# Window attention feeding a channel-mixing layer: probabilities turned over in 32x32 blocks on VectorE, their products with the values on 32x64 parts of the array

## The chip, the cores and the metric

The kernel runs on one core of a Trainium2 chip. The core's engines have their own instruction queues and run beside each other: TensorE (PE in the profile, its weight loads PEld), VectorE (DVE), ScalarE (ACT), GpSimd (POOL) and SyncE (SP, which issues the DMAs here). The metric is the device time of one execution in microseconds. Lower is better.

## The reference

Attention over 8 batches and 8 heads, 512 local and 32 global tokens of head size 64, in fp32. A global query attends to all 544 keys; a local query attends to the 32 global keys (scores `s_lg`) and to local keys at a distance of at most `window` = 32. The result, 8 x 544 tokens of 512 channels, goes through a gated channel-mixing layer in which each token is blended with the one before it.

```python
k_all = np.concatenate([k_g, k_l], axis=2)
v_all = np.concatenate([v_g, v_l], axis=2)
s_g = scale * np.matmul(q_g, k_all.transpose(0, 1, 3, 2))
out_g = np.matmul(sm(s_g), v_all)
mask = np.abs(pos[:, None] - pos[None, :]) <= window
s_ll = np.where(mask, s_ll, -1000000000.0)
s_l = np.concatenate([s_lg, s_ll], axis=-1)
out_l = np.matmul(sm(s_l), np.concatenate([v_g, v_l], axis=2))
...
xk = mu_k * x + (1.0 - mu_k) * x_prev
xr = mu_r * x + (1.0 - mu_r) * x_prev
k = np.maximum(xk @ w_k, 0.0)
v = k * k @ w_v
r = 1.0 / (1.0 + np.exp(-(xr @ w_r)))
return r * v
```

## The kernel before

**Units and blocks.** A unit is one batch and two heads (`Unit`, four per batch); units are worked on in pairs, 16 pairs in all. The 512 local queries are cut into 16 blocks of 32 (`CK`). A block of queries needs a window of four 32-key blocks (`W` = 128 keys): its neighbours, itself and the global block, which is repeated in the order of the keys (`ORDER`, L30) so that every window is a plain slice. There are 14 different windows (`NW`), and two blocks at either end share theirs.

**Scores.** `scores` (L345) makes, for a pair, 128 products on 64x32 parts of the array into four PSUM banks `ps_s`. DVE adds the mask and takes the minimum (L368, one instruction for 128 queries and 128 keys), ACT takes the exponential with the row sum (L374), DVE inverts the sum (L332, L333), POOL multiplies (L380). `scores_global` (L425) does the same for the 2 x 2 x 32 global queries of a pair against 544 keys, in two banks. The probabilities lie in `Pt` and `Pg` with queries on partitions.

**Turning them over.** For the product with the values the keys have to lie on partitions. `transposes` (L407) turns four 128x128 pieces of `Pt` over on TensorE into one PSUM bank `ps_t` (L144), and ACT copies the bank into the tile `PT` (L414, L418). `transposes_global` (L469) does so for `Pg` in six pieces, in two parts, with copies at L478 and L484. In `PT` each group of four query blocks has a row of 128 columns with room behind it (`PITCH`, `TAIL`) for global queries that need the same window.

**Weighted sums.** `weighted` (L488) takes, for each unit, window and head, the window's values as the stationary side (128 keys x 64 channels, a slice of `raw_v`) and the probabilities of all blocks with this window as the moving side, 32, 64 or 96 columns: 112 products for a pair on two column halves of the array, one for each head, into three banks. Each product finishes its output but for the global queries, which add up over the windows. ACT then copies the sums into `xT` and `xg_all` (L529 to L545). The array `v` therefore holds all 14 windows of both heads, 896 KB a unit, laid out on the host.

**The channel-mixing layer.** It works on half a batch of local tokens (`TOK` = 256) at a time. All matrices are split into a high and a low part, so that each product is three matmuls of 128x128 weights with 256 columns (L141, into `ps_m`, three banks). The steps `F` below are 24 such products each. DVE and POOL prepare its inputs (L609 to L619 the blend of a token with the one before; L733 to L741 sums, differences and splits) and take its results (L808 to L835).

**Order.** Up to the loop over the batches (L1183) a scheduler places the instructions; in it TensorE's are kept in program order by hand (`line["on"]`), and those of ACT, DVE and POOL too (`manual_schedule`, L1180). `batch` (L1068) yields the steps of the layer for one batch, `attention` (L876) those of the heads of the next, and `in_turn` (L939) takes them as the string in `BATCH` (L1172) says, A for attention and F for the layer. After an F it also issues one entry of the list `softmaxes`: exponentials and normalising of the pair's scores, spread over the following turns. For a pair the A steps before are four of `transposes`, one for each part of `transposes_global` (the second with the scores of the next pair behind it) and one with the global scores and `weighted`. The first batch goes in halves, with the weights being loaded and decoded beside it.

```python
        None: "AFAFAFAFAF" "AFFAFF" "AFAFAFAFAF" "AFFFAFF",
```

## Time and profile before

| | |
|---|---|
| three runs | 654.7, 662.81 and 659.24 us, median 659.24 |
| the profiled execution | span 655.7 us from its first to its last instruction; its page gives no other time for it |
| mean granted TensorE clock | 0.995 |
| TensorE | busy 96% of the span, 8362 matmuls and as many weight loads |
| transposes of probabilities on TensorE (L144, from `Pt` and `Pg`) | 256 + 16 of 128x128 and 80 of 96 rows |
| weighted sums (from `PT` and `raw_v`) | 1840 products recorded |
| DMA | 127.15 MB, queue of the program busy 54.6% of 16 engines' span |

The profile has several views. The page gives busy time and share of each engine, and groups of instructions with their count, busy time (overlaps counted once), mean duration and the idle time of the engine before them, with what ended it. Mean durations of matmuls contain their way through the array, so they are longer than the spacing of one start to the next. The chain is the work that ended last, followed back from the end. The windows give busy times by stage, and the timeline the instructions in order.

### The profile page before, as it was taken

What the parts mean: (1) busy time and instruction counts of PE and PEld (TensorE: products, weight loads), DVE (VectorE), ACT (ScalarE), POOL (GpSimd) and SP (SyncE); (2) the same over time, 40 slices, a digit from 0 to 9 for tenths busy, and PEclk for the clock granted to TensorE, in tenths of its full rate; (3) what the DMA queues carried; (4) which work ended last, traced back from release to release, by engine and by line L of the source; (5) the groups of instructions that cost most, each with busy time, mean ns of one, the idle gap of its engine ahead of it and who ended that gap; (6) DMA issues with size and microseconds to landing.
All of it is one profiled execution on the core that took longest, in us unless ns stands there. A gap on an engine that the chain in (4) does not pass through costs nothing.

```text
span 655.7 us, 20533 instructions
## 1 busy us (share of the span) xinstructions
PE 630.7 (96%) x8362; PEld 599.6 (91%) x8362; DVE 510.9 (78%) x1308; ACT 338.4 (52%) x1062; POOL 348.4 (53%) x318
## 2 busy tenths in 40 slices
PE   6789899999999989999999999999999999999998
PEld 3567889999989989989999999989999999999997
DVE  4699986556898677986989698986898687787980
ACT  4888686637263576464463727364745533314111
POOL 6377775334856242764357443855366535652840
PEclk9799999999999999999999999999999999999999
DMA  9826534538366922727555584737383562462774
GB/s 333 353 98 241 177 137 163 170 111 307 128 218 208 332 95 73 278 57 289 204 214 190 193 303 163 240 110 267 136 288 103 190 229 67 144 227 79 240 232 170
DMA packets 43565, 127.15 MB, mean 194 GB/s; under 512 B 4048, under 2 KB 20944, under 8 KB 43472
## 3 DMA queue, kind: packets, MB, share of 16 engines
q1 hardware_dynamic: 43472, 125.85, 54.6%
q8 instruction: 66, 1.08, 0.6%
q14 instruction: 27, 0.22, 0.1%
HBM read 108.53 MB, written 17.30 MB: 192 GB/s over the span
## 4 chain that ended last, share of the span: by engine, by line
PE 78%; DVE 10%; DMA 4%; ACT 3%; POOL 2%; issue 2%; SPq 1%; DVEq 0%; ACTq 0%; POOLq 0%
PE ps_m L141 60%; PE ps_s L141 12%; PE ps_t L144 4%; DMA w<-w_k 2%; DMA w<-w_v 1%; DVE diff L614 1%; DVE xfull L582 1%; PE ps_t L141 1%; POOL wv_l L240 1%; ACT Pt L374 1%; DVE a L272 1%; DVE ps_s L230 1%; DVE ps_s L227 1%; DVE kkl L641 1%; DVE bh L740 1%
## 5 line engine op out<-in xcount | busy, mean ns | idle before, releaser
L141 PE MATMUL ps_m<-xkh,wk_h 128*128 128x256 f32 x544 | 155.6, 286 | 2.7 <-DVE gate L685 0.9
L141 PE MATMUL ps_m<-xkl,wk_h 128*128 128x256 f32 x544 | 151.6, 279 | 1.2 <-POOL xkl L587 1.2
L141 PE MATMUL ps_m<-xkh,wk_l 128*128 128x256 f32 x544 | 150.9, 278 | 0.0
L141 PE MATMUL ps_m<-bh,a 128*128 128x256 f32 x736 | 137.3, 283 | 0.0
L380 POOL TENSOR_TENSOR Pt<-Pt,ssum 128x512 f32<-128x512 f32 x64 | 69.6, 1093 | 89.5 <-DVE ssum L333 45.5
L141 PEld LDWEIGHTS ps_m<-bh,a 128*128 128x128 f32 x736 | 115.0, 189 | 0.0
L141 PEld LDWEIGHTS ps_m<-xkh,wk_h 128*128 128x128 f32 x544 | 102.2, 188 | 8.5 <-issue 2.4
L374 ACT ACTIVATE Pt<-Pt,m 128x128 f32<-128x128 f32 x256 | 99.2, 390 | 16.8 <-DVE m L368 16.5
L141 PEld LDWEIGHTS ps_m<-xkl,wk_h 128*128 128x128 f32 x544 | 102.5, 188 | 2.1 <-POOL xkl L587 1.4
L141 PE MATMUL ps_m<-bl,a 128*128 128x256 f32 x368 | 103.0, 280 | 0.0
L141 PEld LDWEIGHTS ps_m<-xkh,wk_l 128*128 128x128 f32 x544 | 102.4, 188 | 0.0
L656 ACT ACTIVATE relu<-ps_m 128x512 f32<-128x512 f32 x52 | 31.0, 596 | 90.3 <-PE ps_m L141 89.8
L141 PE MATMUL ps_m<-xrh,wr_h 128*128 128x256 f32 x272 | 77.0, 283 | 0.0
L141 PE MATMUL ps_m<-xrl,wr_h 128*128 128x256 f32 x272 | 75.6, 278 | 0.0
L141 PE MATMUL ps_m<-xrh,wr_l 128*128 128x256 f32 x272 | 75.4, 278 | 0.0
L619 POOL TENSOR_TENSOR xkl<-xfull,xkh 128x512 fp32r<-128x512 f32 x30 | 39.7, 1325 | 66.5 <-DVE ssum L332 43.1
L141 PEld LDWEIGHTS ps_m<-bl,a 128*128 128x128 f32 x368 | 69.6, 189 | 0.0
L414 ACT COPY PT<-ps_t 128x512 f32<-128x512 f32 x56 | 32.8, 585 | 67.7 <-PE ps_t L144 67.7
L619 POOL TENSOR_TENSOR xrl<-diff,xrh 128x512 fp32r<-128x512 f32 x30 | 40.7, 1356 | 46.8 <-DVE xrh L618 29.8
L368 DVE CUSTOM_DVE_ANT_0 Pt<-ps_s,masks 128x128 f32<-128x128 f32 x256 | 55.9, 285 | 12.0 <-PE ps_s L141 12.0
L141 PE MATMUL ps_s<-raw_qk 64*32 64x128 f32 (+1 forms) x2112 | 55.4, 287 | 5.4 <-DMA raw_qk<-qk 5.4
L741 POOL TENSOR_TENSOR bl<-B,bh 128x512 fp32r<-128x512 f32 x36 | 51.9, 1459 | 14.3 <-DVE bh L740 13.9
(128 smaller groups left out, 1522.1 us busy)
## 6 DMA issues: line engine op xcount, KB each, us to landing
a<-scratch SPq DMA_DIRECT2D x92, 512.0 KB, 4.8
raw_v<-v SPq DMA_DIRECT2D x32, 896.0 KB, 7.6
raw_qk<-qk SPq DMA_DIRECT2D x32, 624.0 KB, 5.5
out_l<-gate SPq DMA_DIRECT2D x32, 256.0 KB, 4.1
w<-w_k SPq DMA_DIRECT2D x8, 512.0 KB, 9.4
w<-w_v SPq DMA_DIRECT2D x8, 512.0 KB, 4.1
w<-w_r SPq DMA_DIRECT2D x4, 512.0 KB, 3.2
scratch<-wv_h SPq DMA_DIRECT2D x8, 256.0 KB, 3.8
```

What stands on the lines that cost most here:

```text
L141: return in_line(nc.tensor.matmul(*a, **kw))
L144: return in_line(nc.tensor.transpose(*a, **kw))
L227: nc.vector.tensor_scalar(bits, word(I32, 1), 3, 0x7FFFFFF8, op0=ALU.logical_shift_left, op1=ALU.bitwise_and)
L230: nc.vector.scalar_tensor_tensor(bits, word(I32, 1), -(2 ** 31), bits, op0=ALU.bitwise_and, op1=ALU.bitwise_or)
L240: engine.tensor_sub(lo, val, hi.bitcast(F32))
L368: read = nc.vector.tensor_tensor_reduce(out=Pt[:, i], in0=place(t, n, h), in1=masks[:, 2 * slots[t][1] + n], op0=ALU.add, op1=ALU.min, sca ...
L374: nc.scalar.activation(Pt[:, i], Pt[:, i], AF.Exp, bias=low_x[:, i:i + 1], scale=-1.0, accum_out=ssum[:, i:i + 1],)
L380: nc.gpsimd.tensor_mul(Pt[:, some], Pt[:, some], inv.unsqueeze(2).to_broadcast([P, 4, W]))
L414: copy(pitched(j, h, 0, 4), tp.rearrange("p (g q) -> p g q", g=4))
L619: nc.gpsimd.tensor_sub(lo[:, both], xf, hi[:, both].bitcast(F32))
L656: nc.scalar.activation(rk, kp, AF.Relu)
L741: (nc.vector if b[0] == "B" else nc.gpsimd).tensor_sub(l, val, h.bitcast(F32))
```

## The change

- **Turning over on VectorE.** `transposes` and `transposes_global` go. `turn_over` transposes `Pt` on DVE straight into `PT`, 128 x 512 in one instruction, and `turn_over_global` all of `Pg` (128 x 544). DVE's transpose works inside blocks of 32x32: block (r, c) of queries and keys stays in its row of blocks, so the keys of a block lie on the partitions 32r to 32r + 31 of the query block's row r. The PSUM bank and ACT's copy between are gone.
- **Products on 32x64 parts.** A key block's product now contracts 32 keys on row quarter r with one head's 64 channels: for each unit 4 groups x 4 key blocks x 4 row quarters x 2 heads, with 32 moving columns, or 64 where the same values also serve a global query block that lies on this quarter. Four key blocks add up in PSUM. Key blocks that a quarter does not have for its global queries (`MORE`, four for each quarter) come as extra products. Row quarter r writes its own bank of `ps_s`, four banks in all.
- **Values.** `v` holds each key block on the row quarters that use it, and the extra blocks: 2304 values a partition in place of 1792, 1152 KB a unit.
- **Copies out.** For each unit ACT copies two pieces for the global queries, one column, and four pieces of local sums.
- **Order.** The scores of the global queries use banks of `t` and `m`. Where the order is by hand, the five transposes of the next pair are spread over the turns after `weighted`, in front of a turn's normalising. The qk loads are issued one pair earlier, after `weighted` and ahead of the v loads. A pair has two A steps there (seven before): the scores, and the global scores with `weighted`; in `BATCH` the five alternating turns become five F.
- **First batch.** Waits for the last transpose become waits for matmuls that keep the clock up (8 and 24 of them).

```diff
+NG = 4
+ROWS = tuple(tuple(NG * g + r for r in range(NG)) for g in range(NG))
+
+
+def blocks_of(i):
+    at = START[window_of(i)] // CK
+    return ORDER[at:at + NG]
+
+
+OWN, MORE = [], []
+for r in range(NG):
+    own = {}
+    for g in range(NG):
+        for n, m in enumerate(blocks_of(ROWS[g][r])):
+            own.setdefault(m, (g, n))
+    MORE.append([m for m in range(NCK) if m not in own])
+    OWN.append({cell: m for m, cell in own.items()})
+CELLS = [m for m in range(NCK - 1)] + [None, NCK - 1]
+N_MORE = max(len(m) for m in MORE)
...
-NV = 2 * NW * D
+PW = 2 * 2 * NG * W
+LV = NG * NG * 2 * D
+NV = LV + N_MORE * D
...
+    PT = const.tile([P, PW + CK * len(CELLS)], F32, name="PT")
...
-        s.v = raw.rearrange("p (h w d) -> p h w d", h=2, d=D)
+        s.v = raw[:, :LV].rearrange("p (g n h d) -> p g n h d", g=NG, n=NG, h=2)
+        s.more = raw[:, LV:].rearrange("p (e d) -> p e d", d=D)
...
+    def part_of(j, h, g=0, n=0):
+        return (((j * 2 + h) * NG + g) * NG + n) * CK
+
+    def turn_over(r, h, j=None):
+
         if j is not None:
-            copy(pitched(j, h, 0, 4), tp.rearrange("p (g q) -> p g q", g=4))
+            at = part_of(j, h)
+            nc.vector.transpose(PT[:, at:at + NG * W], r.Pt[:, 4 * h:4 * h + 4].rearrange("p i w -> p (i w)"))
         else:
-            g0 = 2 * r.slots[0][1]
-            out = PT[:, :, h, g0 * PITCH:(g0 + 2) * PITCH].rearrange("p j (g q) -> p j g q", g=2)[:, :, :, 0:W]
-            copy(out, tp.rearrange("p (j g q) -> p j g q", j=2, g=2))
-        return last
-
+            for t in range(2):
+                at, i = part_of(t, h, 2 * r.slots[0][1]), 4 * h + 2 * t
+                nc.vector.transpose(PT[:, at:at + 2 * W], r.Pt[:, i:i + 2].rearrange("p i w -> p (i w)"))
+
+    def turn_over_global(Pg):
+        nc.vector.transpose(PT[:, PW:], Pg)
...
-    def scores_global(units, bank="o", other="t", later=False):
+    def scores_global(units, bank="t", other="m", later=False):
...
+    def weighted(units, xTs, PG=None, halves=range(2)):
+
+        banks = [psum("s") for _ in range(NG)]
         begun = set()
 
-        def groups(j, of):
-            s = units[j]
-            for w, here, t in GROUPS:
-                here = [i for i in here if i in blocks]
-                t = t if PG else None
-                if not here and t is None or ((here or [None])[0] in alone) != (of is alone):
-                    continue
-                for h in range(2):
-                    P_of, out = PT[:, j, h], (rest if of is alone else sums)[j][h * D:(h + 1) * D]
-                    if len(here) == 1 and t is not None:
-                        i, = here
-                        moving = cells(P_of, PLACE[i], TAIL[t] - PLACE[i], 2)
-                        out = cells(out, of.index(i) * CK, (of.index(None) - of.index(i)) * CK, 2)
-                    else:
-                        x, y = [PLACE[i] for i in here], [of.index(i) * CK for i in here]
-                        if t is not None:
-                            x, y = x + [TAIL[t]], y + [of.index(None) * CK]
-                        n, x, y = len(x) * CK, min(x), min(y)
-                        moving, out = P_of[:, x:x + n], out[:, y:y + n]
-                    first = of is alone or (out.tensor.name, h) not in begun
-                    begun.add((out.tensor.name, h))
-                    last = matmul(out, s.v[:, h, w], moving, start=first, stop=True, skip_group_check=True)
-        groups(0, shared)
-        groups(0, alone)
-        groups(1, alone)
-        groups(1, shared)
+        def product(j, r, h, v, cell, local, m):
+            at, to = [], []
+            if local:
+                at.append(cell)
+                to.append(j * P + cell[0] * CK)
+            if m is not False:
+                at.append(CELLS.index(m))
+                to.append(2 * P + j * CK)
+            at = [part_of(j, h, *x) if isinstance(x, tuple) else PW + x * CK for x in at]
+            rows, out = slice(r * CK, (r + 1) * CK), banks[r][h * D:(h + 1) * D]
+            if len(at) == 2:
+                moving = cells(PT[rows], at[0], at[1] - at[0], 2)
+                out = cells(out, to[0], to[1] - to[0], 2)
+            else:
+                moving, out = PT[rows, at[0]:at[0] + CK], out[:, to[0]:to[0] + CK]
+            matmul(out, v[rows], moving, start=(r, h) not in begun, stop=True, skip_group_check=True)
+            begun.add((r, h))
+        for j, s in enumerate(units):
+            for g in range(NG):
+                local = g // 2 in halves
+                for n in range(NG):
+                    for r in range(NG):
+                        for h in range(2):
+                            m = OWN[r].get((g, n), False) if PG and r == 2 * j + h else False
+                            if local or m is not False:
+                                product(j, r, h, s.v[:, g, n, h], (g, n), local, m)
+            if PG:
+                for e in range(N_MORE):
+                    for h in range(2):
+                        r = 2 * j + h
+                        product(j, r, h, s.more[:, e], None, False, MORE[r][e])
...
+                for h in range(2):
+                    rows = slice(h * D, (h + 1) * D)
+                    nc.scalar.copy(
+                        xg_all[rows, s.c, s.b, 1:SG + 1], banks[2 * j + h][rows, 2 * P + j * CK:2 * P + (j + 1) * CK]
+                    )
+                nc.scalar.copy(xT[:, 0:1], xg_all[:, s.c, s.b, SG:SG + 1])
+            g0, n = NG // 2 * halves[0], NG // 2 * len(halves)
+            for r in range(NG):
+                x = xT[:, 1 + (g0 * NG + r) * CK:]
+                one = x[:, :CK]
+                read = nc.scalar.copy(
+                    bass.AP(one.tensor, one.offset, (one.ap[0], (NG * CK, n), (1, CK))),
+                    banks[r][:, j * P + g0 * CK:j * P + (g0 + n) * CK].rearrange("p (g q) -> p g q", q=CK),
+                )
...
+        for s in pairs[1]:
+            load_qk(s)
+        over = False
+        for pair, nxt, after in zip(pairs, pairs[1:] + [None], pairs[2:] + [None] * 2):
             xTs = [xT_of(s.b, s.c) for s in pair]
-            for s in nxt or ():
-                load_qk(s)
-            for j, r in enumerate(R):
-                for h in range(2):
-                    transposes(r, h, j)
+            by_hand = line["all"]
+            if not over:
+                for j, r in enumerate(R):
+                    for h in range(2):
+                        turn_over(r, h, j)
+                turn_over_global(Pg)
+                if not by_hand:
                     yield
-            transposes_global(Pg, (0,))
-            yield
-            transposes_global(Pg, (1,))
-            by_hand = line["all"]
             if nxt:
                 R = [scores(whole(s), by_hand) for s in nxt]
                 if by_hand:
@@ -908,14 +886,24 @@
             if nxt:
                 Pg, *softmax = scores_global(nxt, later=True)
             copied = weighted(pair, xTs, True)
+            over = by_hand
             if nxt:
                 if by_hand:
-                    softmaxes.append((norm[3], softmax[0]))
-                    softmaxes.append((softmax[1],))
+                    done = 3 - len(softmaxes)
+                    rest = [*softmaxes, (norm[3], softmax[0]), (softmax[1],)] + [()] * 2
+                    turns = [lambda k=k: turn_over(R[k // 2], k % 2, k // 2) for k in range(4)]
+                    turns.append(lambda: turn_over_global(Pg))
+                    for k, f in enumerate(turns):
+                        at = max(k + 1 - done, 0)
+                        rest[at] = (f, *rest[at])
+                    softmaxes.clear()
+                    softmaxes.extend(x for x in rest if x)
                 else:
                     with tc.issue_after(copied.ins):
                         for f in softmax:
                             f()
+            for s in after or ():
+                load_qk(s)
...
+        turn_over_global(Pg[i])
+        warm = keep_warm((8, 24)[i], warm)
+        with tc.issue_after(warm.ins):
...
-        None: "AFAFAFAFAF" "AFFAFF" "AFAFAFAFAF" "AFFFAFF",
+        None: "FFFFF" "AFFAFF" "FFFFF" "AFFFAFF",
...
+    k_all = in_order(k_l, k_g)
+    of_block = lambda m: v_g if m is None else v_l[:, :, m * CK:(m + 1) * CK]
+    v = np.zeros((B, C, NG, CK, NV), v_l.dtype)
+    for r in range(NG):
+        for g in range(NG):
+            for n, m in enumerate(blocks_of(ROWS[g][r])):
+                x = of_block(m).reshape(B, C, 2, CK, D)
+                for h in range(2):
+                    at = ((g * NG + n) * 2 + h) * D
+                    v[:, :, r, :, at:at + D] = x[:, :, h]
+        for e, m in enumerate(MORE[r]):
+            x = of_block(m).reshape(B, C, 2, CK, D)
+            v[:, r // 2::2, r, :, LV + e * D:LV + (e + 1) * D] = x[:, r // 2::2, r % 2]
+    v = v.reshape(B, C, P, NV)
```

More of the change, by code (lines that the diff above doesn't have):

```diff
@@ L463, in cells @@
         return bass.AP(one.tensor, one.offset, (one.ap[0], (step, n), (1, size)))
-    def tails(rows, at, step, n):
-        first = PT[rows, 0, 0, at:at + CK]
-        return bass.AP(first.tensor, first.offset, (first.ap[0], (PART, 4), (step, n), (1, CK)))
-    def transposes_global(Pg, parts=(0, 1), fill=(0, 0)):
-        copies = []
-        for part in parts:
-            ts = ((0, 1, 5), (2, 3, 4))[part]
-            tp = psum("t")[:, :3 * P].rearrange("p (t n) -> p t n", n=P)
-            for n, t in enumerate(ts):
-                lo, hi = (t * (W - CK), (t + 1) * (W - CK)) if t < 5 else (NGK - W, NGK)
-                last = transpose(tp[:hi - lo, n], Pg[:, lo:hi], ident)
-            n, rows = (2 if 5 in ts else 3), slice(0, W - CK)
-            nc.scalar.copy(
-                tails(rows, TAIL[ts[0]], TAIL[ts[1]] - TAIL[ts[0]], n),
-                tp[rows, 0:n].rearrange("p t (u q) -> p u t q", u=4),
-            )
-            if 5 in ts:
-                rows = slice(P - 2 * CK, P)
-                nc.scalar.copy(tails(rows, TAIL[5], CK, 1), tp[rows, 2:3].rearrange("p t (u q) -> p u t q", u=4))
-            last = keep_warm(fill[part], last)
-        return last
@@ L984, in all_transposes @@
         for h in range(2):
-            last = transposes(r, h)
-        return last
+            turn_over(r, h)
     load_qk(heads_0[0])
@@ L1005, in local_global_attention_then_rwkv_ffn @@
     R, Pg = [], []
-    for pair, bank in zip(pairs_0, "os"):
+    for i, pair in enumerate(pairs_0):
         R.append(by_halves(pair, 0))
-        if bank == "o":
-            Pg.append(scores_global(pair, bank, bank))
+        if i == 0:
+            Pg.append(scores_global(pair, "t", "t"))
             keep_warm(10, scores_global.last)
@@ L1012, in local_global_attention_then_rwkv_ffn @@
             with tc.issue_after(keep_warm(16, R[1].made).ins):
-                Pg.append(scores_global(pair, bank, bank))
+                Pg.append(scores_global(pair, "t", "t"))
+        warm = scores_global.last
         next(decoding)
@@ L1016, in local_global_attention_then_rwkv_ffn @@
         all_transposes(R[i])
-        final = transposes_global(Pg[i], fill=((0, 8), (16, 8))[i])
-        with tc.issue_after(final.ins):
+        turn_over_global(Pg[i])
+        warm = keep_warm((8, 24)[i], warm)
+        with tc.issue_after(warm.ins):
             weighted(pair, xTs_0[i], True, (0,))
@@ L1033, in local_global_attention_then_rwkv_ffn @@
     for i, pair in enumerate(pairs_0):
-        final = all_transposes(R[2 + i])
-        with tc.issue_after(final.ins):
-            weighted(pair, xTs_0[i], None, (1,))
+        all_transposes(R[2 + i])
+        weighted(pair, xTs_0[i], None, (1,))
         next(decoding)
```

58 lines of the change are left out of this document (3 added, 55 removed).

## The prediction

> **What bounds the kernel now.** I read the page's busy line first, then the chain of work that ended last in one stretch of the steady part, then busy times by stage.
>
> ```profile
> span 655.7 us, 20533 instructions
> PE 630.7 (96%) x8362; PEld 599.6 (91%) x8362; DVE 510.9 (78%) x1308; ACT 338.4 (52%) x1062; POOL 348.4 (53%) x318
> ```
>
> TensorE is busy for 96% of the span. One pair of units, from its scores to the next pair's, reads in the chain (start, duration, what):
>
> ```profile
> 390.35 1.98 PE ps_s L141 x123
> 392.33 8.37 PE ps_m L141 x72
> 400.70 0.27 PE ps_t L141 x4
> 400.97 4.27 PE ps_s L141 x116
> 405.24 5.66 PE ps_m L141 x48
> 410.89 0.44 PE ps_t L144 x4
> 411.33 2.83 PE ps_m L141 x24
> 414.16 0.44 PE ps_t L144 x4
> 414.60 2.74 PE ps_m L141 x24
> 417.34 0.44 PE ps_t L144 x4
> 417.77 2.83 PE ps_m L141 x24
> 420.61 0.44 PE ps_t L144 x4
> 421.04 2.74 PE ps_m L141 x24
> 423.79 0.33 PE ps_t L144 x3
> 424.11 2.74 PE ps_m L141 x24
> 426.85 0.33 PE ps_t L144 x3
> 427.18 1.98 PE ps_s L141 x127
> ```
>
> There is nothing but TensorE in it, so here each microsecond off TensorE's queue is a microsecond off the kernel, until another engine takes over. The transposes (L144) stand in that queue six times: 4 x 0.44 + 2 x 0.33 = 2.42 us per pair. The 4.27 us hold the global scores and the weighted sums; the sums alone appear in the last pair, which has no successor (the 3.61 us row below).
>
> Who could take over? The windows give span, then busy PE, PEld, DVE, ACT, POOL:
>
> ```profile
> 0.00:109.00 109.00, 92.45 (x1375) 76.92 (x1375) 88.90 (x277) 82.13 (x265) 74.86 (x102) 0.97 0.60 224
> 109.00:154.00 45.00, 44.98 (x769) 42.75 (x769) 23.45 (x104) 22.18 (x87) 16.19 (x15) 1.00 0.39 134
> 154.00:226.70 72.70, 71.61 (x1001) 68.92 (x997) 57.90 (x150) 35.17 (x114) 43.27 (x39) 1.00 0.68 238
> 226.70:284.40 57.70, 54.17 (x659) 52.08 (x660) 47.51 (x107) 34.10 (x105) 29.13 (x23) 1.00 0.45 158
> 261.30:284.40 23.10, 22.15 (x198) 21.78 (x198) 22.54 (x36) 11.21 (x31) 18.10 (x14) 1.00 0.72 250
> 390.35:462.00 71.65, 71.16 (x998) 68.67 (x998) 59.73 (x159) 38.32 (x126) 38.48 (x30) 1.00 0.59 207
> ```
>
> The last row is one whole batch (two pairs) of the steady part: TensorE full, DVE 59.73 of 71.65 us. DVE is the second bound, and the change gives it work.
>
> **The change part by part.**
>
> ```profile
> 541.20 3.61 PE ps_s L141 x112
> L141 PE MATMUL ps_s<-PT,raw_v 128*64 128x32 f32 x896 | 28.2, 222 | 0.4 <-DVE m L368 0.4
> L141 PE MATMUL ps_s<-PT,raw_v 128*64 128x64 f32 x448 | 18.1, 222 | 0.2 <-issue 0.2
> L414 ACT COPY PT<-ps_t 128x512 f32<-128x512 f32 x56 | 32.8, 585 | 67.7 <-PE ps_t L144 67.7
> L822 DVE TENSOR_TENSOR sum<-ps_m,sum 128x512 f32<-128x512 f32 x6 | 4.1, 691 | 13.1 <-PE ps_m L141 13.1
> L741 DVE TENSOR_TENSOR bl<-B,bh 128x512 fp32r<-128x512 f32 x40 | 53.2, 1331 | 1.4
> L380 POOL TENSOR_TENSOR Pt<-Pt,ssum 128x512 f32<-128x512 f32 x64 | 69.6, 1093 | 89.5 <-DVE ssum L333 45.5 <-ACT Pt L374 21.6 <-PE ps_t L141 10.6
> ```
>
> *Transposes leave TensorE*: -2.42 us per pair, all of it on the path. With them go the ACT copies out of ps_t (0.585 us each); ACT is busy 38.32 of 71.65 us, so this counts as nothing.
>
> *Weighted sums*. Before: 112 products in 3.61 us, two column halves at a time, 32.2 ns each. After, by the code: per unit 4 groups x 4 key blocks x 4 row quarters x 2 heads = 128, and 4 extra blocks x 2 heads = 8; two units, 272. No row shows a product on a 32x64 part. Lower end: a half takes 64.5 ns per product now, and eight parts working freely give 64.5 / 8 = 8.1 ns, 2.2 us in all. Upper end: no more overlap than today, 272 x 32.2 ns = 8.8 us. The nearest row is that of the scores: they also use eight parts (64x32) and need 1.98 us for the code's 128 products (127 recorded), 15.5 ns each. I take that: 272 x 15.5 ns = 4.21 us, +0.60 us per pair, net -1.82. The same two rows show that halving the width saves nothing: products 32 and 64 wide both take 222 ns. [...]
>
> *Transposes come to DVE*: per pair four of 128x512 and one of 128x544. Before has no such row. Nearest with one pass over 512 elements: 691 ns (L822, reads PSUM). Far end: 1331 ns, an operation from SBUF to SBUF that lies beside POOL. Below 691 lies half of it, if DVE moved two elements at a time. I take 0.69 and 0.73 us, so 3.5 us per pair, 7.0 per batch. [...]
>
> DVE would then need 59.73 + 7.0 = 66.7 us per batch; TensorE 71.65 - 2 x 1.82 = 68.0. What DVE idles now is mostly waiting, and later work takes those gaps only where it is late anyway:
>
> ```profile
> 373.97 0.43 DVE L618 CAST xrh<-diff 128x512 fp32r<-128x512 f32 x1 [2.62 <-PE ps_m L141]
> 377.36 0.69 DVE L822 TENSOR_TENSOR sum<-ps_m,sum 128x512 f32<-128x512 f32 x1 [2.66 <-PE ps_m L141]
> 396.67 0.29 DVE L368 CUSTOM_DVE_ANT_0 Pt<-ps_s,masks 128x128 f32<-128x128 f32 x1
> ```
>
> In the first pair of a batch the transposes fall right into the 2.62 and 2.66 us that DVE waits for TensorE; in the second DVE runs on without such a gap. I leave 2.0 us of the 11.9 idle us that DVE cannot fill: 68.7 us per batch, DVE setting it, a gain of 2.95. Bounds: 68.0 and 71.65.
>
> *New waits*. A transpose waits for POOL's normalising (1093 ns) and blocks everything behind it on DVE, among it the additions that free ps_m. The order in the diff puts it one turn of 24 products (2.74 us) behind that multiplication, so I charge nothing; without that cover it is up to 1.1 us for each of five. The weighted sums now write all four ps_s banks from the start, so they wait for all sixteen reductions L368. These ended at 396.96, the sums began after 400.97: 4 us of cover, gone if DVE falls that far behind. One ps_m bank serves the global scores; it is free again after a short DVE read.
>
> ```profile
> PE ps_t L144 <- ACT PT L418: 5.3, 2, 4.5
> PE ps_t L144 <- POOL Pt L380: 3.4, 2, 2.1
> ```
>
> TensorE's own waits for the softmax (these two rows) go, since no transpose stands in its line; what is late next is the weighted sum, several products later.
>
> *DMA, SP's queue*. `v` grows from 896 to 1152 KB, and qk loads move one pair forward, ahead of the v loads. In the steady part a pair has over 30 us to land: nothing. At the start two v loads go out ahead of the third weight chunk:
>
> ```profile
> raw_v<-v SPq DMA_DIRECT2D x32, 896.0 KB, 7.6
> GB/s 333 353 98 241 177 137 163 170 111 307 128 218 208 332 95 73 278 57 289 204 214 190 193 303 163 240 110 267 136 288 103 190 229 67 144 227 79 240 232 170
> 4.94 14.89 DMA w<-w_k
> ```
>
> 512 KB more at 340 GB/s (first two slices) is 1.5 us on a chunk that is on the chain. POOL loses its clearing of PT, and ACT has four more small copies per pair: hidden by idle ACT.
>
> **The sum**, against the 655.7 us span. 0 to 109: +1.5 for DMA; DVE, busy 88.90 of 109, takes some 7 us more of half-size transposes, of which I charge 2, less 1.5 for TensorE's waits on ACT's copy: +2.0 (ends -4, +7). 109 to 154: two pairs, DVE half idle: 2 x -1.82 = -3.6. 154 to 226.7: two pairs, but the first one's five transposes stand together before its scores; half of 3.5 us comes back: -2.0. 226.7 on: two pairs, TensorE's wait for POOL saves another 1.5, and in 261.3 to 284.4, where DVE is full (22.54 of 23.10), 3.5 us come straight on: -1.5. The last seven pairs, 3.5 batches: 3.5 x -2.95 = -10.3. After 541.20 nothing. Sum -15.4: span 640.3. The median of the runs, 659.24, stands 3.5 above the profiled span; so 643.8 us.
>
> **The rivals.**
> - *DVE eats the gain.* It falls so far behind that the gaps are not found again: the last seven pairs, and those from 154 to 284, gain nothing. For it: 22.54 of 23.10. Against: the two gaps above. -3.6 + 2.0 gives a span of 654.1, 657.6 us.
> - *Slower: parts do not overlap.* 8.8 us in place of 3.61 is +5.2 - 2.42 = +2.7 per pair, 14 pairs and the start: about +40, 699 us. It turns slower once a product takes over (3.61 + 2.42) / 272 = 22 ns. Against it: 15.5 ns in the scores.
> - *Slower: DVE's transposes share a path with POOL* and cost 1.33 us as L741 does: a batch needs 59.73 + 13.4 + 2.0 = 75.1, +3.5 each, +12 over 3.5 batches; 154 to 226.7 +1, the next +3, the start +6, 109 to 154 -3.6: about +19, 678 us. It turns slower above (71.65 - 2.0 - 59.73) / 10 = 0.99 us.
> - *More: eight parts run freely*, 2.2 us: TensorE gains 3.8 per pair, DVE still holds the steady part at -10.3; -7.6, -4, -3.5 and +2 elsewhere: -23.4, 635.8 us.
>
> **How the numbers follow.** Two per cent (13 us: faster below 646.1, slower above 672.4) is about what a measurement of this kernel can tell from no change. My forecast has 0.47 (its own range 636 to 653, about 0.12 of it on the near side of 646), more 0.13, DVE eats the gain 0.24, DVE beside POOL 0.11, no overlap 0.05. Faster 0.35 + 0.13 = 0.48; same 0.12 + 0.24 = 0.36; slower 0.16. From 634 to 672 leaves out half of "more" (0.06) and nearly all that is slower (0.14).
>
> **What would show it.** Right: no L144 but the warm-up ones, weighted sums of about 4.2 us, DVE transposes of 0.65 to 0.75 us, batches of about 68.7 us with DVE over 95% busy, and chain pieces on DVE where there are none now. Wrong: transposes near 1.3 us beside POOL; weighted sums over 6 us; TensorE waiting for ps_s before the sums; DVE still idle while batches last 68.0, which would say that its waits gave way more than I allow.

## The result and the profile after

The changed kernel takes 875.54 us (median of four runs, 874.0 to 876.42), beside 660.8 us for the kernel before in the same measurement (654.7 to 662.81): ratio 1.3291, 95% interval 1.3203 to 1.338. The prediction was 643.8 us, in a range of 634 to 672. It was wrong, and by more than its slowest rival (699).

The page of the changed kernel, its head and the lines of the queues, the chain and one group:

```profile
span 873.9 us, 33725 instructions
PE 722.6 (83%) x14970; PEld 685.3 (78%) x14970; DVE 538.5 (62%) x1396; ACT 301.2 (34%) x1018; POOL 345.2 (40%) x312
...
PEclk9666786969796978879696978969696979789999
...
q8 instruction: 117, 1.92, 0.8%
...
PE 71%; issue 16%; DVE 7%; DMA 3%; ACT 2%; POOL 1%; SPq 0%; DVEq 0%; ACTq 0%; POOLq 0%
...
L150 PE MATMUL ps_s<-PT,raw_v 32*64 32x32 f32 (+1 forms) x8800 | 153.9, 266 | 121.6 <-issue 117.1
```

No engine took over: every engine is busy for a smaller share than before, TensorE 83% in place of 96%. The new piece of the chain is "issue", 16% of the span: an engine waits, and for nothing that the profile shows. The group says where: 117.1 us of it stand in front of the weighted sums. Two counts are to be noted. The sums have 8800 records (a record is one matmul in the trace, with its weight load), where the code has 4400 products. And the kernel has 13,192 instructions more (33725 - 20533), while the queue that brings instructions moves 0.84 MB more than before:

```profile
q8 instruction: 66, 1.08, 0.6%
```

That is 64 bytes for each new instruction (0.84 MB / 13,192), and the bytes are those of TensorE alone: its 2 x 14970 loads and matmuls at 64 bytes make the 1.92 MB. A packet of it holds 16.4 KB (1.92 MB / 117).

The timeline of TensorE through one pair's weighted sums in the changed kernel (start, duration, line, operation, count, and in brackets the idle time before with what ended it):

```profile
461.47 2.11 PE L150 MATMUL ps_s<-PT,raw_v 32*64 32x64 f32 x183
467.43 2.67 PE L150 MATMUL ps_s<-PT,raw_v 32*64 32x64 f32 x128 [3.85 <-issue]
471.18 2.14 PE L150 MATMUL ps_s<-PT,raw_v 32*64 32x32 f32 x128 [1.07 <-issue]
476.29 2.45 PE L150 MATMUL ps_s<-PT,raw_v 32*64 32x32 f32 x105 [2.97 <-issue]
```

The stage takes 17.27 us where 4.21 were forecast and 3.63 stood. It has 544 records for 272 products. TensorE runs 183 of them at 11.5 ns, stops for nearly 4 us, and from then on works in portions of exactly 128 records. A record is a weight load and a matmul, so a portion is 256 instructions, 16 KB at 64 bytes each: one packet. In the stretch from 461 to 479 us the queue has four packets, which make 0.07 MB:

```profile
q8 instruction: 4, 0.07, 1.4%
DMA  0005679999960000100009089999600000001000
```

The second line is the busy share of the DMA engines in 40 slices of 0.45 us, in tenths. The packets start at 465.0, 468.5, 474.0 and 477.4 us. The three portions (467.43, 471.18 and 476.29) each begin 2.3 to 2.7 us after one of the first three. The third packet comes 5.4 us after the second: from about 471.4 to 474 us the kernel's own loads keep the DMA engines full.

The windows of the same stretch (span, then busy PE, PEld, DVE, ACT, POOL with counts, granted clock, DMA share, GB/s): the first burst, the rest of the sums, and the 168 feed-forward products behind them.

```profile
461.47:463.58 2.11, 2.11 (x185) 2.01 (x184) 1.73 (x3) 1.89 (x9) 1.29 (x2) 1.00 0.41 84
463.58:478.68 15.10, 7.21 (x362) 6.91 (x361) 2.71 (x11) 0.81 (x5) 2.26 (x2) 0.55 0.42 156
478.68:499.60 20.92, 20.92 (x169) 20.82 (x168) 19.17 (x31) 6.54 (x19) 14.15 (x10) 0.91 0.63 220
```

While TensorE stops and goes, the granted clock falls to 0.55, and the feed-forward products behind it still pay: 20.92 us for 168, where the chain before had 8.37 us for 72, or 19.5 for as many. It takes no long gap for that: in a later stage of the same kernel, where no gap is longer than 1.88 us, the clock falls too.

```profile
705.84:708.57 2.73, 2.73 (x246) 2.61 (x245) 2.61 (x6) 1.93 (x9) 1.77 (x2) 1.00 0.03 9
710.44:714.18 3.74, 2.31 (x128) 2.15 (x128) 3.08 (x6) 0.00 (x0) 1.51 (x2) 0.57 0.48 160
```

What came out as forecast are VectorE's transposes:

```profile
L419 DVE STREAM_TRANSPOSE PT<-Pt 128x512 f32<-128x512 f32 x56 | 37.4, 693 | 22.4 <-PE ps_s L150 21.0 <-POOL xkl L596 1.4
L426 DVE STREAM_TRANSPOSE PT<-Pg 128x544 f32<-128x544 f32 x16 | 11.7, 732 | 5.0 <-PE ps_s L150 4.5 <-POOL Pg L459 0.5
```

To place the loss, the span is cut at the starts of the weighted sums of pair 3 (the first that is not halved), of pair 5 (the first in the part ordered by hand) and of pair 16, the last. This table holds the runs below as well; us, from the timelines.

| kernel | to pair 3 | 3 to 5 | 5 to 16 | behind | span |
|---|---|---|---|---|---|
| before | 92.2 | 58.3 | 390.6 | 114.6 | 655.7 |
| changed | 122.9 | 89.6 | 537.9 | 123.5 | 873.9 |
| no_turn | 98.0 | 54.7 | 371.0 | 114.5 | 638.2 |
| quarter | 108.8 | 66.1 | 390.9 | 110.0 | 675.8 |
| quarter_noturn | 96.1 | 62.6 | 379.9 | 110.0 | 648.6 |
| quarter_warm | 106.2 | 65.9 | 384.2 | 109.4 | 665.7 |
| spread | 122.3 | 76.6 | 438.6 | 136.0 | 773.5 |

The loss is everywhere: 31 us ahead of pair 3, 31 in the next two pairs, 147 in the eleven after that (13.4 each), 9 behind. Each row is one execution: no_turn leaves the code ahead of pair 3 as it was and reaches it 5.8 us later than before, so differences of that size in the first column say nothing.

### The profile page after: what moved, and what is told of

Same layout as the page of the kernel before. It is cut to its first block, busy times and chain, and to the rows that moved or that the text cites. A ratio compares the mean times of both kernels' runs of the same rounds, so it can differ in the third digit from the quotient of the medians.

```text
span 873.9 us, 33725 instructions
## 1 busy us (share of the span) xinstructions
PE 722.6 (83%) x14970; PEld 685.3 (78%) x14970; DVE 538.5 (62%) x1396; ACT 301.2 (34%) x1018; POOL 345.2 (40%) x312
## 3 DMA queue, kind: packets, MB, share of 16 engines
q8 instruction: 117, 1.92, 0.8%
## 4 chain that ended last, share of the span: by engine, by line
PE 71%; issue 16%; DVE 7%; DMA 3%; ACT 2%; POOL 1%; SPq 0%; DVEq 0%; ACTq 0%; POOLq 0%
PE ps_m L150 50%; PE ps_s L150 19%; ACT Pt L382 1%; PE ps_t L150 1%; DVE bl L718 1%; DMA w<-w_k 1%; DVE diff L591 1%; DMA w<-w_v 1%; DVE Pt L376 1%; DMA a<-scratch 1%; DVE PT L419 1%; DVE a L279 0%; PE ps_m L153 0%; DMA w<-w_r 0%; POOL wk_l L247 0%
## 5 line engine op out<-in xcount | busy, mean ns | idle before, releaser
L150 PE MATMUL ps_s<-PT,raw_v 32*64 32x32 f32 (+1 forms) x8800 | 153.9, 266 | 121.6 <-issue 117.1
L150 PEld LDWEIGHTS ps_s<-PT,raw_v 32*64 32x64 f32 x8800 | 144.6, 173 | 138.7 <-issue 128.5
L150 PE MATMUL ps_m<-bh,a 128*128 128x256 f32 x736 | 130.5, 278 | 0.4 <-DMA a<-scratch 0.3
L150 PEld LDWEIGHTS ps_m<-xkh,wk_h 128*128 128x128 f32 x544 | 107.7, 198 | 8.1 <-DVE gate L662 4.3
L150 PEld LDWEIGHTS ps_m<-xkl,wk_h 128*128 128x128 f32 x544 | 108.0, 198 | 0.3 <-POOL xkl L596 0.3
L150 PE MATMUL ps_m<-xrh,wr_h 128*128 128x256 f32 x272 | 88.6, 326 | 2.1 <-ACT wr_h L246 1.5
L150 PE MATMUL ps_m<-xrl,wr_h 128*128 128x256 f32 x272 | 86.3, 317 | 0.0
L150 PE MATMUL ps_m<-xrh,wr_l 128*128 128x256 f32 x272 | 85.6, 316 | 0.0
L586 DVE TENSOR_TENSOR diff<-xT 128x256 f32<-128x256 f32 x56 | 36.0, 674 | 76.2 <-ACT xT L519 74.2
L511 ACT COPY xg_all<-ps_s 64x32 f32<-64x32 f32 x64 | 11.7, 183 | 185.3 <-PE ps_s L150 184.7
```

The source lines that it names most:

```text
L150: return in_line(nc.tensor.matmul(*a, **kw))
L511: nc.scalar.copy(xg_all[rows, s.c, s.b, 1:SG + 1], banks[2 * j + h][rows, 2 * P + j * CK:2 * P + (j + 1) * CK])
L586: nc.vector.tensor_sub(self.shape(d[:, j]), self.cur(c0 + j), self.prev(c0 + j))
```

## The experiments

The theory: TensorE runs out of instructions. They come in blocks of 256, some 4 us apart, and a long run of short products uses a block up in about 2 us. The rival: products on 32-row parts of the array are slow in themselves. A second question was why the trace has two records for each product of the sums.

**A quarter of the products.** Three of the four key blocks are left out of the weighted sums.

```diff
-                for n in range(NG):
+                for n in range(1):
```

> The changed kernel with one key block (the first) of each group of queries in the weighted sums instead of four; three quarters of the sums' local products are left out, so 80 products per pair stay (160 recorded load/matmul pairs instead of 544). Supply theory (TensorE runs out of fetched instructions after some 180 pairs, then gets 128 pairs per 4.4 us): 160 pairs lie below the 183 that came in one go, so the sums take 160 x 11.5 to 16 ns = 1.8 to 2.6 us in one burst without an idle gap above 1 us, the clock stays near 1 behind them, and the kernel takes 620 to 650 us. Rival (each 32-row product is slow in itself, 17.27 us / 544 = 32 ns per pair, also without a gap): 160 x 32 = 5.1 us per stage, a burst evenly spaced, and about 660 us.

Measured: 677.67 us, beside 659.86 for the kernel before. In the stages the theory holds; the first line below is the usual picture, 15 ns for a record and no gap. The second and third are another pair:

```profile
428.88 2.40 PE L150 MATMUL ps_s<-PT,raw_v 32*64 32x64 f32 x160
...
248.50 2.38 PE L150 MATMUL ps_s<-PT,raw_v 32*64 32x64 f32 x131
255.03 1.31 PE L150 MATMUL ps_s<-PT,raw_v 32*64 32x32 f32 x29 [4.16 <-issue]
```

The same products on the same parts run at full pace in one pair, and in another stop for 4.16 us after 131. The time itself was missed by both theory (620 to 650 us) and rival (about 660): the theory had taken over the rest of the prediction. The table says where: 16.6 us late by pair 3, 7.8 more by pair 5, and nothing gained in the eleven pairs after that, where 1.5 us each were forecast. That is a second error, followed up below.

**Scores issued four times.** The kernel before, with each local score product issued four times to the same place; nothing of the change is in it.

```diff
+                        for _ in range(4):
                             last = matmul(
```

> The kernel before, each local score product on 64 rows x 32 columns issued four times in a row to the same place: nothing of the change is in it, only 512 load/matmul pairs stand together where 128 stood. Supply theory: the first 180 or so at 16 ns = 2.9 us, the other 330 at 4.4 us per 128 = 11.4 us, so a stage that took 2.05 us takes about 14 us, in bursts of 128 with idle gaps put down to issue; some 16 stages, those that already waited for banks gain less: 800 to 850 us. Rival (products on 32-row parts are what is slow, 64-row ones are not): 4 x 2.05 = 8.2 us per stage, no gaps, 740 to 760 us.

Measured: 1093.46 us, more than either theory, at a clock of 1.0, and with no gap. The stage was bound by something else:

```profile
L141 PE MATMUL ps_s<-raw_qk 64*32 64x128 f32 x8192 | 496.0, 273 | 4.6 <-DMA raw_qk<-qk 4.6
```

With the same part of the array four times in a row, and the same place for the result, a record takes 496.0 us / 8192 = 61 ns; rotating over eight parts it took 16. At 61 ns 128 records last 7.8 us, and the instructions come in time. The run didn't test the theory; it shows that such repeats don't overlap, and not whether the part or the place of the result keeps them from it. So the whole set was repeated instead, product by product:

```diff
+        for _ in range(4):
             for t, (s, p) in enumerate(slots):
```

> The kernel before with its whole set of local score products issued four times over, set after set, so that each product follows one on another of the eight 64x32 parts, as in the kernel before (where the same product came four times in a row, each took 59 us / 1000 on its own part). Nothing of the change is in it. Supply theory: the first 180 or so at 16 ns = 2.9 us, the other 330 at 4.4 us per 128 = 11.4 us: about 14 us in a stage that stood at 2.05 us, in bursts of 128 with idle gaps put down to issue, and 790 to 850 us. Rival (what starves TensorE belongs to products on 32 rows): 4 x 2.05 = 8.2 us per stage without gaps, 740 to 760 us.

Measured: 845.18 us, beside 655.77. One stage of it, and its windows:

```profile
442.01 3.73 PE L141 MATMUL ps_s<-raw_qk 64*32 64x128 f32 x250
447.06 2.07 PE L141 MATMUL ps_s<-raw_qk 64*32 64x128 f32 x128 [1.32 <-issue]
451.08 2.02 PE L141 MATMUL ps_s<-raw_qk 64*32 64x128 f32 x128 [1.95 <-issue]
454.82 0.42 PE L141 MATMUL ps_s<-raw_qk 64*32 64x128 f32 x6 [1.73 <-issue]
```

```profile
442.01:455.24 13.23, 8.24 (x514) 7.22 (x513) 4.97 (x22) 3.08 (x11) 0.00 (x0) 1.00 0.18 63
```

Bursts of 128 and gaps that end with "issue", 13.23 us where TensorE's own work is 8.24: the starvation is there without the change, on parts of another shape. The first burst was longer than expected (250 records, not 180), and a portion came every 3.9 us on the average rather than 4.4. Here the clock stays at 1.00, with gaps under 2 us; in the changed kernel it falls, with gaps of 3.85 us and also of 1.88, so the length of the gaps alone doesn't decide it. What else does is not shown.

How often a portion came went with the load of the DMA engines. In the changed kernel, from the start of a full portion of 128 records to the start of the next one, 3.45 to 4.02 us pass where the engines are nearly idle (share up to 0.05; five cases, at clocks from 0.50 to 0.94), and 3.73 to 5.94 us, mostly over 4, where their share is 0.45 or more (17 cases). In another stage of this run, from 401.83 us on, where the instruction queue alone moved, it was 3.74 and 3.73 us. So the supply was slower while the kernel's own loads moved. No run moved the loads away to test the cause.

**The same products, spread.** All work of the changed kernel is kept; in the part ordered by hand the 272 products of a pair are issued in six slices with feed-forward steps between them, and VectorE's turning follows the last slice.

```diff
-            copied = weighted(pair, xTs, True)
+                for copied in weighted(pair, xTs, True, slices=SLICES):
+                    if copied is None:
+                        yield False
...
-        None: "FFFFF" "AFFAFF" "FFFFF" "AFFFAFF",
+        None: "AFFAFAFAFAFAFA" "FFF" "AFFAFAFAFAFAFA" "FF",
```

> The changed kernel with all its products, but the 272 of a pair issued in six slices with feed-forward steps of 128x256 products between them (in the part ordered by hand). Supply theory: a pair needs some 1,800 instructions, 7.1 blocks of 256 at 4.4 us = 31 us, while TensorE has 33 to 34 us of work in it, so fetching runs ahead under the long products: a slice of 90 pairs takes 1.5 us without gaps, the half clock goes, and the kernel takes 640 to 700 us. Rival (the products are slow in themselves): the same 17 us per pair split in six, about 870 us.

Measured: 774.91 us, ratio 1.1727 to the kernel before (1.1669 to 1.1785): 100 us less than the changed kernel, but outside what either expected. Two pairs (440 to 521 us), the windows and TensorE's waits in them, and the six slices of an earlier pair:

```profile
440.14:521.40 81.26, 78.29 (x1821) 73.59 (x1819) 63.09 (x169) 33.85 (x122) 38.49 (x31) 0.98 0.56 195
```

```profile
PE ps_m L150 <- DVE sum L819: 2.2, 1, 2.2
PE ps_s L150 <- issue: 0.8, 2, 0.5
```

```profile
360.25 1.19 PE L150 MATMUL ps_s<-PT,raw_v 32*64 32x64 f32 x90
364.39 1.08 PE L150 MATMUL ps_s<-PT,raw_v 32*64 32x32 f32 x81
366.91 0.34 PE L150 MATMUL ps_s<-PT,raw_v 32*64 32x32 f32 x9 [1.45 <-issue]
370.12 1.43 PE L150 MATMUL ps_s<-PT,raw_v 32*64 32x32 f32 x92
375.44 1.15 PE L150 MATMUL ps_s<-PT,raw_v 32*64 32x32 f32 x90
379.78 1.16 PE L150 MATMUL ps_s<-PT,raw_v 32*64 32x32 f32 x90
383.79 1.50 PE L150 MATMUL ps_s<-PT,raw_v 32*64 32x32 f32 x92
```

Where the slices are, starvation is nearly gone: 0.8 us in these two pairs, 14.1 in all from pair 5 on (90.2 there in the changed kernel), and the clock is back at 0.98. The same number of records as in the changed kernel, in the same order, takes 7.85 us a pair in place of 17 (the seven bursts added up). TensorE is busy for 78.29 of 81.26 us, where the kernel before had 71.16 of 71.65. The sums of a pair before:

```profile
293.17 3.63 PE L141 MATMUL ps_s<-PT,raw_v 128*64 128x96 f32 x112
```

So 4.2 us a pair are more work in the sums (7.85 - 3.63), and 2.42 of transposes are saved: 1.8 net. With slices a pair still loses 4.4 ((438.6 - 390.6) / 11). Another 1.2 are stops that end with "issue" (13.6 us up to pair 16, ahead of the sums and the steps behind them); the other 1.4 are not accounted for, the clock of 0.98 in place of 1.00 among them. Ahead of pair 5 the sums still stand in one piece, and that part still starves (26.9 us, as in the changed kernel).

**What doubles a product.** First 64 rows in place of 32 (each sums over two quarters, so half as many products).

```diff
-            rows, out = slice(r * CK, (r + 1) * CK), banks[r][h * D:(h + 1) * D]
+            rows, out = slice(r // 2 * D, (r // 2 + 1) * D), banks[r][h * D:(h + 1) * D]
...
+                            here = local and r % 2 == n % 2
```

> The changed kernel with products on 64 rows x 64 columns of the array instead of 32 x 64, half as many local ones: 169 products per pair where there were 272 (each sums over two quarters, so the sums are not those of the reference). If it is the 32 rows that double a product: 169 records per pair, 169 x 15 to 30 ns = 2.6 to 5.1 us in one burst without a gap, and 670 to 690 us, as with a quarter of the products. If the doubling belongs to the operands' form or to the second column half: 338 records, more than the 183 that came in one go, so a gap of 3 to 5 us, some 8 us per stage, and 740 us or more.

Measured: 782.95 us; 338 records for the 169 products, with a gap:

```profile
422.15 3.22 PE L150 MATMUL ps_s<-PT,raw_v 64*64 64x64 f32 x166
427.20 5.87 PE L150 MATMUL ps_s<-PT,raw_v 64*64 64x32 f32 x172 [1.83 <-issue]
```

The 32 rows are not the cause. Next the columns: products of 32 columns in the changed kernel (each covers half of the value columns), and in the kernel before, there with all the work kept by splitting each product in two.

```diff
-                    last = matmul(out, s.v[:, h, w], moving, start=first, stop=True, skip_group_check=True)
+                    for cols in (slice(0, CK), slice(CK, D)):
+                        last = matmul(out[cols], s.v[:, h, w, cols], moving, start=first, stop=True, skip_group_check=True)
```

> The changed kernel with each of the 272 products per pair on 32 rows x 32 columns (one half of the value columns for even key blocks, the other for odd ones; the other halves of the products are left out). Theory of the doubling, formed after products on 64 rows stayed double: an fp32 product is issued twice when it has 64 columns and once when it has 32, whatever its rows. Then 272 records per pair in place of 544: the first 180 or so at 15 ns, one gap of 2 to 4 us, the last 90: 6 to 9 us per stage, 730 to 770 us. Rival (the doubling belongs to these products' operands or to their accumulating): 544 records again, some 17 us per stage, 860 us or more.

> The kernel before with each weighted sum's product split into two of 32 columns (128x32 parts in place of 128x64), all of the work kept, nothing else changed. If 64 columns are what doubles a record, the count stays at 112 per pair and the products rotate over four parts in place of two: 112 x 16 ns = 1.8 us in place of 3.63, -1.8 us for each of 16 pairs, at most -29 us where TensorE is the bound: 630 to 645 us. Rivals: the halves are issued twice as well, 224 records, 3.6 to 7.3 us per stage, 660 to 720 us; or parts of 128 rows do not overlap and the time stays at 655 to 662 us.

> As the run before it, and the two global score products of 64 columns x 480 keys split into columns of 32 as well. If halves on four parts overlap: the global scores take 0.5 us in place of 0.98, some 0.5 us per pair more, at most -8 us against the run before it. If they do not: the same time within 3 us.

Measured: 851.98 us for the first, with all 8800 records:

```profile
L150 PE MATMUL ps_s<-PT,raw_v 32*32 32x32 f32 x7232 | 114.1, 224 | 110.0 <-issue 108.2 <-DVE w L240 0.9 <-DVE m L376 0.8
L150 PE MATMUL ps_s<-PT,raw_v 32*32 32x64 f32 x1568 | 98.3, 266 | 27.5 <-issue 25.6 <-DVE PT L426 1.8
```

703.1 us for the second, ratio 1.0625 (1.0538 to 1.0712), and 718.51 for the third, ratio 1.0842 (1.0765 to 1.0919). The theory of the columns fell: in the first two the rival of twice the records came true. The third, which was expected to be level with the second or up to 8 us faster, is 15 us slower; its global scores have twice the records too (128 over 480 keys in place of 64). In two pairs of the second run:

```profile
516.51 2.96 PE L141 MATMUL ps_s<-PT,raw_v 128*32 128x96 f32 x224
```

```profile
432.49 2.35 PE L141 MATMUL ps_s<-PT,raw_v 128*32 128x96 f32 x184
438.88 1.40 PE L141 MATMUL ps_s<-PT,raw_v 128*32 128x64 f32 x40 [4.04 <-issue]
```

The 112 split products of a pair were already 56 in the code (14 windows x 2 heads x 2 units), and 112 in the trace; now they are 112 and 224. On four parts in place of two they run in 2.96 us, less than the 3.63 before, and the kernel still loses 6%: in other pairs the same 224 records stop on the way, above for 4.04 us behind 184. Such stops ahead of the sums add up to 28.1 us of the 45.2 that the span is longer (700.9 - 655.7); the clock is lower too (0.961 in place of 0.995). This led back to the code of the scores and to their row in the kernel before:

```profile
L141 PE MATMUL ps_s<-raw_qk 64*32 64x128 f32 x2048 | 39.6, 279 | 5.4 <-DMA raw_qk<-qk 5.4
```

`t`, `n`, `r_` and `h` make 2 x 2 x 4 x 2 = 32 products a call and 64 a pair; 2048 for 16 pairs is 128. **Every fp32 product of either kernel that was counted stands twice in the trace, whatever its shape; the feed-forward products (in fp32r) and the transposes stand once** (272 of `xrh` with `wr_h`, 4 x 4 for each of 17 blocks of tokens; 256 of `Pt`, 16 for each of 16 pairs). The 128 and 112 "products" of the description and the prediction are records; the code has 64 and 56.

**The rest of the prediction: what turning over costs where.** The kernel before without TensorE's transposes and their copies in the part ordered by hand (the turning over is left out there).

```diff
+        if line["all"]:
+            return None
```

> The kernel before without TensorE's transposes of the probabilities and their copies in the part whose order is written by hand (seven pairs; the turning over is left out there, and the sums read older probabilities). If the transposes lie on the path: -7 x 2.42 = -17 us. If VectorE takes the gain as it did in one rival: -10 us or less. If they were hidden: 0.

Measured: 636.1 us, ratio 0.9626 (0.9572 to 0.968), 21 to 28 us off; the profiled executions differ by 17.5 (655.7 - 638.2), and the one without transposes is the slowest of its four. That the 17.5 meet the -17 expected is an accident: the part ordered by hand holds twelve pairs and not seven, as the transposes that are left show (64 of 256, so four pairs of 16).

```profile
L144 PE MATMUL ps_t<-ident,Pt 128*128 128x128 f32 x64 | 9.3, 276 | 1.6 <-issue 1.6
```

In the table the eleven pairs from 5 to 16 gain 19.6 us, 1.8 each, where 2.42 would be all. In these executions TensorE's transposes are on the path for three quarters of their time; the medians of the runs lie further apart than the two executions (23.8 us).

Then the quarter kernel without VectorE's transposes.

> The kernel with one key block of four in the weighted sums (677.67 us), and without VectorE's transposes (the turning over is left out, the sums read zeros). With a quarter of the products the seven pairs ordered by hand went as predicted, but the first 150 us took 27 us more than in the kernel before. If VectorE's 4 to 5 transposes per pair (3.5 us) hold up the start: 640 to 655 us, with most of the 27 us gone. If it is the order of the other work there (POOL's Pt ahead of the decoding of weights, the half clock after idle gaps): 665 us or more, and the first 150 us as before within 5 us.

Measured: 650.39 us, 27 less than with them. VectorE's turning over is not free: to pair 3 it costs 12.7 us (108.8 - 96.1), from 3 to 5 3.5, and from 5 to 16 11.0, or 1.0 a pair, of the 3.5 us that it takes. The 12.7 are twice the 5.8 us by which the same start differed between two executions; the 3.5 are no more than single executions differ by (before and no_turn by 3.6 there).

Last, the half clock in the start: 40 more filler transposes on TensorE in the quarter kernel, just ahead of the second pair's first sums.

```diff
-        warm = keep_warm((8, 24)[i], warm)
+        warm = keep_warm((8, 64)[i], warm)
```

> The kernel with one key block of four in the weighted sums (677.67 us; the other blocks' products are left out), with 40 more filler transposes on TensorE right ahead of the second pair's first sums, where TensorE stood idle for 4.95 us from 29.3 us on and then ran at half clock from 34.2 to 51.5 us. If the half clock is what the start loses beside VectorE's transposes: the granted clock between 34 and 51 us is 0.9 or more, the 13.7 us of TensorE's work there shrink by 4 to 6 us, and the time is 668 to 674 us. If TensorE's pace isn't what the start waits for (VectorE and the decoding of weights are): the clock rises, and the time stays at 675 to 681 us.

Measured: 667.44 us, beside 665.5 for the kernel before in that measurement. The clock from 34.2 to 51.5 us rose from 0.50 to 0.74, less than wanted:

```profile
34.20:51.50 17.30, 10.18 (x211) 8.23 (x210) 11.32 (x36) 6.83 (x32) 7.99 (x7) 0.74 0.19 63
```

Pair 3 starts only 2.6 us earlier, less than two executions of one start can differ. With the clock raised to 0.74 only, no large effect of the half clock is seen. The larger part of the gain comes behind pair 5 (6.7 us), and one place of it is the pair that had stopped for 4.16 us above:

```profile
244.90 2.69 PE L150 MATMUL ps_s<-PT,raw_v 32*64 32x64 f32 x160
```

The gap is gone, though nothing near it was changed; 40 transposes ahead, 80 instructions, have moved it against the blocks of 256, and the work before it differs in time. The runs don't part the two from each other or from the loads. Whether anything else makes pair 3 late (96.1 without VectorE's transposes, 92.2 before) can't be said from single executions.

No run that does all the work beat the kernel before.

## Why the prediction was wrong, step by step

**The step that failed is the term "272 x 15.5 ns = 4.21 us" of the weighted sums**, in two places.

- *The price.* 15.5 ns was read off as 1.98 us for "the code's 128 products". The code has 64; 128 are records. So a product on one of eight rotating parts costs 31 ns, and 272 cost 8.4 us: the slices of spread show 7.85. The old sums were counted in records as well (112), the new ones in products (272), and the two were compared. The trace of before held the answer: counting the loops of `scores` against x2048 would have shown it. With 31 ns the step reads +4.8 - 2.42 = +2.4 us per pair, above the 22 ns at which the prediction's own rival turns slower: it is that rival's 699 us in size, though its reason, parts that don't overlap, is not the cause (records on eight parts do overlap: 61 ns in a row on one part, 16 in rotation).
- *The limit.* Neither bound (2.2 and 8.8 us) held the 17.27 us, since both price the array, and the array was not the limit. (Counted in records, the upper one would be 544 x 32.2 ns = 17.5 us. That it meets 17.27 is chance: in the bursts of that stage a record takes 11.5 to 23 ns.) 544 records are 1,088 instructions; before, the longest run of such records was 128 for the scores and 112 for the sums. The queue's row was on the page (1.08 MB in 66 packets) and wasn't used. From pair 5 to 16 the sum now nearly closes: +4.2 work, -2.4 transposes, +9.1 of standing and slow pace (the stages of pairs 5 to 15 last 17.0 us on the average, less 7.85), +1.4 of lower clock behind them, if the stage shown is typical: 12.3 of the 13.4 us a pair.

The wait for a portion was as long as 4.8 us in one place of the changed kernel. On the clock, 0.55 was granted behind a gap of 3.85 us and 1.00 in the scores with gaps below 2, but 0.57 and then 0.50 (714.18 to 718 us) in the sums with gaps of at most 1.88.

**TensorE's transposes: nearly right.** -2.42 us per pair was forecast, "all of it on the path"; 1.8 came through in the profiled executions when they alone were taken out.

**VectorE's transposes: the duration right, the cover too thin.** 0.69 and 0.73 us were forecast, 693 and 732 ns came, with no slowing beside POOL (128x512: 698 ns for the 26 with POOL busy for over half of their time, 691 for the 27 with POOL busy for under a tenth); that rival falls. The gain of 2.95 us a batch did not come: with a quarter of the products pairs 5 to 16 gained nothing, and with 40 fillers, which took some stops out, 6.4 us, 1.2 a batch. The windows of one batch with a quarter of the products, first with the turning and then without it:

```profile
428.90:498.70 69.80, 66.06 (x1053) 62.79 (x1051) 63.01 (x169) 33.66 (x122) 38.30 (x30) 0.98 0.62 227
```

```profile
406.90:475.30 68.40, 65.77 (x1051) 62.77 (x1049) 59.71 (x159) 33.49 (x121) 38.36 (x30) 0.98 0.63 231
```

VectorE is busy 63.01 of 69.80 us here, and idles 6.8; I had allowed 2.0. Its busy time is 3.3 us above the 59.71 without the turning, where 7.0 were added in the sum: other instructions of it take less beside the transposes (the blend written to `diff` 811 ns on the average, 985 without them). The runs don't say why. This batch is 1.40 us longer with the turning than without, at the same work of TensorE (66.06 and 65.77). TensorE idles 3.7 us here and still 2.6 without the turning, so the turning is the smaller part of what holds it, and the larger stays open. That VectorE eats the gain, as the rival has it, is neither shown nor ruled out.

**The start: the sign right, the size not.** +2.0 us up to 109 us was forecast, with ends of -4 and +7. The changed kernel is 30.7 us late by pair 3; even with a quarter of the products it is 16.6. Without VectorE's turning 12.7 of these are gone, where it was charged with 2; the difference of two executions is uncertain by some 6 us.

**Copies, loads, new waits.** No wait of TensorE is put down to ACT's copies out of the sums in the changed kernel. The loads of `v` were charged with nothing in the steady part as well. That left out the supply of instructions: while loads moved, the blocks came later, as the portions above show (3.73 to 5.94 us in place of 3.45 to 4.02). What the 256 KB more a unit add to this is not measured. The wait for all banks of `ps_s` ahead of the sums hardly appears: 1.1 us for "DVE m L376" in the whole changed kernel.

## What to carry to other kernels

Count an operation in the code and in the trace before taking its price from a row: an fp32 product here was two records, and a rate "per product" was half of what it cost. Many small products on many parts spend instructions: the sums split over four parts took 2.96 us in place of 3.63 where nothing stopped them, and the kernel with their 224 records in place of 112 lost 6%. Work out instructions per microsecond against the rate at which a long run of them was ever delivered here, 256 in 3.45 us at best and in 3.73 to 5.94 with a DMA share of 0.45 or more, and put long products between the short ones (stops of 90.2 us fell to 14.1 from pair 5 on). Short runs help only in part: 160 records at a time still stopped in some pairs, once for 4.16 us. Where a stage has idle time "issue" on TensorE between bursts of equal count, read the instruction queue before the semaphores.

## What the runs showed of the hardware

- Instructions of TensorE came in portions of 256 (128 records of load and matmul), for parts of 32x64 and of 64x32 alike; in the changed kernel one every 3.45 to 4.02 us with a DMA share of up to 0.05 and every 3.73 to 5.94 with one of 0.45 or more. At a clock of 0.50 they came as fast (3.47 us) as at 0.94 (3.45).
- In the changed kernel the 49 portions behind a stop of over 0.6 us each began 2.2 to 2.7 us after a packet of the instruction queue started. How many records ran ahead of the first stop varied: 131 (quarter), 166 (64 rows), 183 (changed), 184 (the split sums of the kernel before), 231 and 250 (the scores in rotation).
- fp32 products stood in the trace as two load and matmul pairs each, on parts of 128x64 (112 for 56 of a pair), 128x32 (224 for 112), 64x64 (338 for 169), 64x32 (128 for 64), 32x64 (544 for 272) and 32x32 (8800 for 4400 in all).
- Products in a row on one 64x32 part, to one place, took 61 ns a record, in rotation over eight parts 16; in rotation over 32x64 parts 11.5 (183 in 2.11 us, at a clock of 1.00) to 15 (160 in 2.40 us, quarter).
- With stops in a row the granted clock fell to 0.50 in the sums even where no stop was longer than 1.88 us (705.84 to 719.72 us of the changed kernel); in a stage of the scores in rotation it stayed at 1.00 with stops of 1.32 to 1.95.
- VectorE's transposes in 32x32 blocks of fp32 took 693 ns for 128x512 and 732 for 128x544.
